# Top-k attention with a rational feed-forward: a cubic written as a line times a shifted square, weight bits on ScalarE, reciprocals on VectorE

## The chip, the core and the metric

The kernel runs on one core of a Trainium2 chip. The metric is device time in microseconds (us) of one launch. The core has five engines that each work through a fixed list of instructions in order: TensorE (PE in the profile, its weight loads PEld), VectorE (DVE), ScalarE (ACT), GpSimd (POOL) and SyncE (SP), which issues the transfers (DMA).

## What is computed

For 8 batches of 8 heads with 576 rows of 64, the attention keeps the 32 largest scores of each row; its output feeds a layer with a rational activation. The two weights arrive as float64.

```python
scores = scale * np.matmul(q, k.transpose(0, 1, 3, 2))
kth = np.partition(scores, -top_k, axis=-1)[..., -top_k:-top_k + 1]
scores = np.where(scores >= kth, scores, -1000000000.0)
scores = scores - np.max(scores, axis=-1, keepdims=True)
attn = np.exp(scores)
attn = attn / (np.sum(attn, axis=-1, keepdims=True) + 1e-09)
x = np.matmul(attn, v)                      # then laid out as 4608 x 512
h = x @ w_in                                # w_in 512 x 2048
h2 = h * h
h3 = h2 * h
P = a[0] + a[1] * h + a[2] * h2 + a[3] * h3
Q = 1.0 + np.abs(b[0]) * np.abs(h) + np.abs(b[1]) * h2
g = P / (Q + 1e-6)
out = g @ w_out                             # w_out 2048 x 512
```

## The kernel before

**Tiles.** The attention is cut into 288 tiles of 128 rows by 576 scores (32 of them hold the last 64 rows of two heads). A unit is two tiles, one for each head of a pair, or one such mixed tile; there are 160 units. For a tile TensorE computes the scores (L616), ScalarE copies them out of PSUM (`sb`, L623), VectorE folds the two halves into their maxima and minima (`hi`, L634, `lo`, L627) and takes the top 32 by repeated MAX and MATCH_REPLACE (L645, L653), ScalarE takes the exponentials (`e`, L684), and VectorE keeps those above the 32nd and sums them (`pr` and `ss`, L687). For a unit the sum then gets 1e-9 added (`guard`, L277 or L275 by engine), is inverted (`inverse`, L746, on GpSimd as a power of -1), is spread over 128 columns (`widen`, `rw`, L283 or L281), and is transposed with the probabilities on TensorE (L768, L770); the products with v (`av`, L794) are multiplied by it (L813).

**Feed-forward.** 256 rows make a chunk (18 of them), and a chunk takes 8 groups of 256 hidden columns. Each operand of a product is split in a high and a low part, and three products are added: `ph` (L943) for a group's hidden values, `po` (L1109) for the output. Between the two, a group's 128 x 512 values pass through ScalarE and GpSimd. There are two forms. The 15 first chunks (120 groups) use four evictions from PSUM by ScalarE (`square`, `p1`, `size`, `p3`), two GpSimd operations for the cubic (`p2`, L969, and `p4`, L975), and three ScalarE passes for 1/Q: the square of a shifted |h| (`rise`), Ln, and Exp of its negative. The 3 last chunks (24 groups, `y.late`) use three evictions and a Horner scheme, with `slope`, `curve`, `horner2`, `horner1` and `horner0` (L277, L1023, L1026, L1030 on VectorE; L1034, L1035 on GpSimd). Then both split the result into `g` (L277 or L275) and `gl` (L1007, GpSimd).

**Weights.** 32 blocks of 128 x 512 float64 are loaded as pairs of 32-bit words (`w_w`) while the attention is already running. For each half of a block ScalarE takes the sign of the high word (L422), VectorE shifts the high word into a PSUM tile (`high`, L427) and joins the top bits of the low word (`low`, L434), ScalarE takes the size (L440), GpSimd multiplies by the sign (L444), and the block is split in two (L460).

**Order.** A planner in the kernel (`Plan`) places every step: it holds lengths for each engine, keys for urgency (table `KEY`), and rings of buffers, and it writes the instructions down in the order in which its own clock starts them. Each engine then runs its list in order and waits where an input is not there. A second program for all data (`full`) follows behind a test of flags; it runs when `unfit` or one of the flags is above zero.

## Time and profile before

| | |
|---|---|
| median of 3 runs | 1566.55 us (1564.59 to 1568.24) |
| the profiled execution | 1566.08 us, of which the trace's span is 1564.3 us |
| busy: TensorE, its weight loads | 1416.2 us (91%), 1183.0 us (76%) |
| busy: VectorE | 1446.5 us (92%) |
| busy: ScalarE | 1306.3 us (84%) |
| busy: GpSimd | 1325.1 us (85%) |

Busy time is a union over an engine's instructions. Instructions of one engine overlap a little (the end of one is written back while the next runs), so a group's mean length is some hundredths of a microsecond above what it keeps the engine for.

### The profile page before, as it was taken

What the parts mean: (1) busy time and instruction counts of PE and PEld (TensorE: products, weight loads), DVE (VectorE), ACT (ScalarE), POOL (GpSimd) and SP (SyncE); (2) the same over time, 40 slices, a digit from 0 to 9 for tenths busy, and PEclk for the clock granted to TensorE, in tenths of its full rate; (3) what the DMA queues carried; (4) which work ended last, traced back from release to release, by engine and by line L of the source; (5) the groups of instructions that cost most, each with busy time, mean ns of one, the idle gap of its engine ahead of it and who ended that gap; (6) DMA issues with size and microseconds to landing.
All of it is one profiled execution on the core that took longest, in us unless ns stands there. A gap on an engine that the chain in (4) does not pass through costs nothing.

```text
span 1564.3 us, 32666 instructions
## 1 busy us (share of the span) xinstructions
PE 1416.2 (91%) x9729; PEld 1183.0 (76%) x9729; DVE 1446.5 (92%) x4548; ACT 1306.3 (84%) x2587; POOL 1325.1 (85%) x1893
## 2 busy tenths in 40 slices
PE   2547876998999999899999999999999999999998
PEld 1335655787788788788788888888888888887796
DVE  6998989999999999899999999999999999999773
...
GB/s 211 233 185 206 189 169 232 210 133 204 222 190 172 177 227 210 175 179 227 227 191 173 200 208 247 171 188 214 230 171 170 224 209 192 178 177 131 166 206 129
DMA packets 175004, 303.23 MB, mean 194 GB/s; under 512 B 26080, under 2 KB 80352, under 8 KB 174816
## 3 DMA queue, kind: packets, MB, share of 16 engines
...
q14 instruction: 108, 0.88, 0.2%
q0 software_dynamic: 64, 0.00, 0.0%
...
## 4 chain that ended last, share of the span: by engine, by line
PE 45%; DVE 16%; POOL 15%; ACT 9%; DMA 6%; issue 5%; SPq 3%; POOLq 0%; ACTq 0%; DVEq 0%
PE ph_m L943 13%; PE po_m L1109 12%; PE av L794 8%; PE s L616 5%; DVE m L645 5%; PE trp L768 4%; DVE hi L653 4%; DVE pr L687 2%; DMA wi_m<-win_l 2%; POOL ss L746 2%; DVE hi L634 2%; ACT sb L623 2%; DVE lo L627 1%; POOL gl_m L1007 1%; ACT p L780 1%
## 5 line engine op out<-in xcount | busy, mean ns | idle before, releaser
L645 DVE MAX8 m<-hi 128x8 f32<-128x288 f32 (+1 forms) x1152 | 500.6, 454 | 0.8
L653 DVE MATCH_REPLACE8 hi<-m,hi 128x288 f32<-128x288 f32 x864 | 380.2, 445 | 0.0
L943 PE MATMUL ph_m<-xh_m,win_h 128*128 128x256 f32 x1024 | 305.5, 298 | 4.3 <-ACT p L780 4.2
L943 PE MATMUL ph_m<-xh_m,wi_m 128*128 128x256 f32 x1024 | 292.1, 285 | 3.8 <-DMA wi_m<-win_l 3.8
L943 PE MATMUL ph_m<-xl_m,win_h 128*128 128x256 f32 x1024 | 290.5, 284 | 0.0
L768 PE MATMUL trp<-ident,pr 128*128 128x128 f32 x1312 | 227.6, 285 | 67.8 <-DVE pr L687 26.5
L780 ACT COPY p<-trp 128x512 f32<-128x512 f32 (+1 forms) x448 | 230.1, 519 | 39.9 <-PE trp L768 24.5
L768 PEld LDWEIGHTS trp<-ident,pr 128*128 128x128 f32 x1312 | 164.7, 145 | 108.7 <-ACT w_w L440 29.3
L687 DVE SCALAR_TENSOR_TENSOR pr<-sb,m,e 128x576 f32<-128x576 f32 x288 | 230.5, 800 | 2.6 <-ACT e L684 1.6
L684 ACT ACTIVATE e<-sb,st 128x576 f32<-128x576 f32 x288 | 219.1, 761 | 11.4 <-DVE pr L687 7.8
L623 ACT COPY sb<-s 128x576 f32<-128x576 f32 x288 | 186.6, 648 | 41.8 <-PE s L616 32.4
L1109 PE MATMUL po_m<-wout,g_m 128*128 128x512 f32 x512 | 217.9, 426 | 1.0 <-ACT ob_t L1127 1.0
L943 PEld LDWEIGHTS ph_m<-xh_m,win_h 128*128 128x128 f32 x1024 | 197.4, 193 | 14.6 <-ACT p L780 7.9
L1109 PE MATMUL po_m<-wout,gl_m 128*128 128x512 f32 x512 | 204.0, 399 | 3.7 <-POOL gl_m L1007 3.7
L1109 PE MATMUL po_m<-wl_m,g_m 128*128 128x512 f32 x512 | 203.7, 398 | 0.0
L943 PEld LDWEIGHTS ph_m<-xh_m,wi_m 128*128 128x128 f32 x1024 | 193.6, 189 | 4.4 <-DMA wi_m<-win_l 4.4
L943 PEld LDWEIGHTS ph_m<-xl_m,win_h 128*128 128x128 f32 x1024 | 194.8, 190 | 2.3
L794 PE MATMUL av<-p,vm 128*64 128x256 f32 (+1 forms) x1920 | 193.4, 351 | 3.4 <-ACT p L780 2.1
L1007 POOL TENSOR_TENSOR gl_m<-pa_m,g_m 128x512 fp32r<-128x512 f32 x128 | 168.2, 1314 | 4.5
L794 PEld LDWEIGHTS av<-p,vm 128*64 128x64 f32 x1920 | 114.3, 145 | 75.0 <-issue 17.1
L634 DVE TENSOR_TENSOR hi<-s,sb 128x288 f32<-128x288 f32 x288 | 128.6, 447 | 38.9 <-ACT sb L623 26.8
L969 POOL TENSOR_TENSOR pa_m<-pa_m,hh_m 128x512 f32<-128x512 f32 x112 | 144.9, 1294 | 21.2 <-ACT pa_m L966 20.8
(144 smaller groups left out, 3539.8 us busy)
## 6 DMA issues: line engine op xcount, KB each, us to landing
wl_m<-wout_l SPq DMA_DIRECT2D x256, 256.0 KB, 3.4
wi_m<-win_l SPq DMA_DIRECT2D x128, 512.0 KB, 4.2
...
q<-qx SPq DMA_DIRECT2D x128, 128.0 KB, 2.6
q<-qx SPq DMA_DIRECT2D x256, 64.0 KB, 2.1
...
```

Of the source, the lines that this page charges most:

```text
L623: nc.scalar.copy(t.sb, t.s[:, :, 0:HF])
L634: nc.vector.tensor_tensor(t.hi, t.s[:, 0, 0:HF], t.sb[:, 1], ALU.max)
L645: nc.vector.max(to, t.both if not full and o == 24 else getattr(t, src))
L653: nc.vector.match_replace(x, t.m[:, o : o + 8], x, NEG)
L684: nc.scalar.activation(t.e, t.sb, AF.Exp, scale=SCALE, bias=t.st)
L687: nc.vector.scalar_tensor_tensor(out=t.pr, in0=t.sb, scalar=t.kth, in1=t.e, op0=ALU.is_ge, op1=ALU.mult, accum_out=u.ss[:, t.h : t.h + 1],)
L768: nc.tensor.transpose(u.ps[i][:, c * P : (c + 1) * P], u.pr[:, x], ident)
L780: nc.scalar.copy(pair.pT[i][:, at].rearrange("p c n -> p (c n)"), u.ps[i][:, 0 : n * P])
L794: nc.tensor.matmul(pair.av[d, 0 : u.nq * len(pair.units)], lhs, x[:, 0, d] if u.mixed else x[:, 0] if lone else x, start=(c == 0), stop=(c ...
L943: nc.tensor.matmul(y.ph[:, f * NT : (f + 1) * NT], w, z[:, c, :], start=(c == 0 and i == 0), stop=(c == HP - 1 and i == 2),)
L1007: engine().tensor_tensor(out=tile_("gl", F32R), in0=y.pa, in1=y.g.bitcast(F32), op=ALU.subtract)
L1109: nc.tensor.matmul(o.po[i], z, w, start=(ff == 0 and n == 0), stop=(ff == NF - 1 and n == 2),)
```

## The change

1. **The cubic.** With a root r of the cubic found on the chip, P(h) = (a3 h - a3 r) ((h + t)^2 + f). A group has one eviction as a Square with a bias (`curve`), one as a line (`line`), one as |h| (`size`), and one step `cubic` = (curve + f) * line, which GpSimd does in two instructions (L1084, L1085) and VectorE could do in one. All 144 groups take this form; the late form is gone, and `slope`, `horner2`, `horner1`, `horner0` with it.
2. **Coefficients.** `add_coefficients` puts the root's Newton steps and a test of how well the form fits into the plan: 68 GpSimd instructions of one column, 11 on VectorE, 8 on ScalarE. The 11 one-column instructions that VectorE had for this at the start are gone.
3. **Weight bits.** `ends3` on ScalarE reads the low word as an unsigned number, scales it and adds 2, which leaves its top bits in place; VectorE's `merge` joins the shifted high word. The step `high` on VectorE is gone (64 instructions); ScalarE has 64 more of 128 x 256. The PSUM tile of the first eight blocks comes from another ring (`o` for `mm`), and a block takes three buffers for four.
4. **Reciprocals.** `inverse` is a RECIPROCAL on VectorE (160 instructions) for the power on GpSimd.
5. **Planner.** New lengths and keys, and small delays (`later`) that it assumes behind the guard, the reciprocal and loads. The products on TensorE and the transfers are the same in number.

```diff
@@ the weights
-                def high(i=i, place_bits=place_bits):
+                def ends3(i=i, place_bits=place_bits):
                     es, low, high, size_ = o.raw[i]
-                    nc.vector.tensor_scalar(
-                        place_bits(), high, 3, 0x40000000,
-                        op0=ALU.logical_shift_left, op1=ALU.bitwise_xor,
+                    nc.scalar.activation(
+                        place_bits().bitcast(F32), low.bitcast(U32), AF.Identity, scale=THREE, bias=toggle
                     )
-                def low(i=i):
+                def merge(i=i):
                     es, low, high, size_ = o.raw[i]
                     nc.vector.scalar_tensor_tensor(
-                        o.bits[i], low, 29, o.bits[i], op0=ALU.logical_shift_right, op1=ALU.bitwise_or
+                        o.bits[i], high, 3, o.bits[i], op0=ALU.logical_shift_left, op1=ALU.bitwise_xor
                     )
...
-                s2 = add("DVE", 0.33, high, [s1], key + 1, take=[bits_hold])
-                s3 = add("DVE", 0.36, low, [s2], key + 1)
+                s2 = add("ACT", act(256, 1), ends3, [ld], key + 1, take=[bits_hold])
+                s3 = add("DVE", 0.36, merge, [s1, s2], key + 1)
@@ the coefficients
+    def add_coefficients(key):
...
+        def over(o, x):
+            to("DVE", 0.16, lambda: nc.vector.reciprocal(o, x))
...
+        over(over_tilt, slope0)
+        ts((zero, a0, over_tilt, None, m, None))
+        for i in range(5):
+            value = (
+                (value0, zero, a3, a2, m, p), (value0, value0, zero, a1, m, p), (value0, value0, zero, a0, m, p),
+            )
+            ts(*value, (tilt, zero, slope2, slope1, m, p), (tilt, tilt, zero, slope0, m, p))
+            over(over_tilt, tilt)
+            ts((zero, value0, over_tilt, zero, m, p))
...
+        to("DVE", 0.16, lambda: nc.vector.tensor_tensor(unfit, unfit, outer, ALU.max))
+        return last[0]
@@ a unit's reciprocal
         def inverse():
-            x = u.ss[:, 0:nr]
-            if plan.at == "DVE":
-                nc.vector.reciprocal(x, x)
-            else:
-                nc.gpsimd.tensor_tensor(out=x, in0=x, in1=minus[:, 0:nr], op=ALU.pow)
+            nc.vector.reciprocal(u.ss[:, 0:nr], u.ss[:, 0:nr])
...
-        inv = add({**small(KEY["NM"]), "POOL": 0.27}, None, guard, [t1], key + KEY['URG'])
-        inv = add("DVE", 0.085, inverse, [inv], key + KEY['URG']) if full else add(
-            "POOL", KEY['PW'], inverse, [inv], key + KEY['URG'])
+        inv = add({**small(KEY["NM"]), "POOL": 0.27}, None, guard, [t1], key + KEY['URG'], later=0.12)
+        inv = add("DVE", 0.085, inverse, [inv], key + KEY['URG'], later=KEY['IL'])
@@ a group
+        def curve():
+            nc.scalar.activation(tile_("pa"), y.ph, AF.Square, bias=turn)
+        def line():
+            nc.scalar.activation(tile_("hh"), y.ph, AF.Identity, scale=a3, bias=near)
+        def cubic():
+            add_mult(y.pa, flat, y.hh)
...
+            e1 = add("ACT", act(512, 1), curve, [last, prev.e], ku, give=[mm], take=took)
+            s1 = add("ACT", act(512, 2), line, [e1], ku + 0.1, give=[mm])
+            e2 = add("ACT", act(512), size, [e1], ku + 0.2, give=[mm])
+            s3 = add(fused(512, *KEY['p2']), None, cubic, [s1, e1], k2 + 0.3, give=[th["hh"]])
+            s4 = add("ACT", act_sb(512, 2), rise, [e2], k2 + KEY['RI'])
```

Where instructions stand now, at three places. In the rows a line is that of its own kernel, and a name ends in batch, row block, pair and a buffer number.

**GpSimd, start of the program.** Behind the constants GpSimd had the first query block (`qx`), the first keys (`kh`, `kl`), and the first weights (`w_w0`, on lines L444 and L460):

```order
L277 TENSOR_SCALAR qx_0_0_0_145<-qx_0_0_0_145 128x256
L558 TENSOR_TENSOR qx_0_0_0_145<-qx_0_0_0_145 128x256
L277 TENSOR_SCALAR kh_0_0_166<-kl_0_0_149 128x576
L515 TENSOR_TENSOR kl_0_0_149<-kl_0_0_149,kh_0_0_166 128x576
L444 TENSOR_TENSOR w_w0_2_155<-w_w0_0_151,w_w0_2_155 128x256
L444 TENSOR_TENSOR w_w0_2_155<-w_w0_1_153,w_w0_2_155 128x256
L460 TENSOR_TENSOR w_w0_3_156<-w_w0_2_155,win_h_95 128x512
```

Now coefficients (`cf`, from the loaded `co`) stand ahead of the first keys and between all that follows:

```order
L485 TENSOR_SCALAR cf_73<-cf_73 128x1
L483 TENSOR_SCALAR cf_73<-co_70 128x1 x3
L281 TENSOR_SCALAR kh_0_0_162<-kl_0_0_131 128x576
L483 TENSOR_SCALAR cf_73<-co_70,cf_73 128x1
L588 TENSOR_TENSOR kl_0_0_131<-kl_0_0_131,kh_0_0_162 128x576
L485 TENSOR_SCALAR cf_73<-cf_73,co_70 128x1 x3
L485 TENSOR_SCALAR cf_73<-cf_73 128x1 x2
L281 TENSOR_SCALAR qx_0_0_0_154<-qx_0_0_0_154 128x256
L485 TENSOR_SCALAR cf_73<-cf_73 128x1
L631 TENSOR_TENSOR qx_0_0_0_154<-qx_0_0_0_154 128x256
L485 TENSOR_SCALAR cf_73<-cf_73,co_70 128x1 x3
L485 TENSOR_SCALAR cf_73<-cf_73 128x1 x2
```

Twelve coefficient instructions stand ahead of `kh` (the last four of them open this piece), and the query block has moved behind the keys.

**VectorE, start.** Before, the order was four weight instructions, the eleven for the coefficients, and then the first tile's `hi`. Now it is this, with `cf` the reciprocals of the root search:

```order
L489 RECIPROCAL cf_73<-cf_73 128x1 x5
L429 SCALAR_TENSOR_TENSOR w_w0_b0_184<-w_w0_0_156,w_w0_b0_184 128x256
L429 SCALAR_TENSOR_TENSOR w_w0_b1_193<-w_w0_1_158,w_w0_b1_193 128x256
L489 RECIPROCAL cf_73<-cf_73 128x1 x3
L707 TENSOR_TENSOR hi_0_0_0_246<-s_0_0_0_0_230,sb_0_0_0_0_239 128x288
L700 TENSOR_TENSOR lo_0_0_0_0_250<-s_0_0_0_0_230,sb_0_0_0_0_239 128x288
L718 MAX m_0_0_0_252<-hi_0_0_0_246 128x8
L489 RECIPROCAL cf_73<-cf_73 128x1
L726 MATCH_REPLACE hi_0_0_0_246<-m_0_0_0_252,hi_0_0_0_246 128x288
```

Eight reciprocals stand ahead of the first `hi`, each with its input from GpSimd, and a ninth two rows behind it.

**VectorE and GpSimd around one unit (batch 4, row block 1, pair 2).** Before, VectorE went from the last tile of the unit (`pr_4_1_2`) straight through the next tile:

```order
L687 SCALAR_TENSOR_TENSOR pr_4_1_2_12155,ss_4_1_2_12156<-sb_4_1_2_1_12145,m_4_1_2_12111,e_4_1_2_1_12231 128x576
L645 MAX m_4_0_3_12264<-hi_4_0_3_12236 128x8
L634 TENSOR_TENSOR hi_4_0_3_12236<-s_4_0_3_1_12259,sb_4_0_3_1_12277 128x288
L653 MATCH_REPLACE hi_4_0_3_12236<-m_4_0_3_12264,hi_4_0_3_12236 128x288
L627 TENSOR_TENSOR lo_4_0_3_1_12333<-s_4_0_3_1_12259,sb_4_0_3_1_12277 128x288
L645 MAX m_4_0_3_12264<-hi_4_0_3_12236 128x8 x2
L653 MATCH_REPLACE hi_4_0_3_12236<-m_4_0_3_12264,hi_4_0_3_12236 128x288 x2
```

Now the unit's reciprocal stands between the next tile's operations:

```order
L760 SCALAR_TENSOR_TENSOR pr_4_1_2_12048,ss_4_1_2_12049<-sb_4_1_2_1_12006,m_4_1_2_11994,e_4_1_2_1_12125 128x576
L718 MAX m_4_0_3_12150<-hi_4_0_3_12123 128x8
L707 TENSOR_TENSOR hi_4_0_3_12123<-s_4_0_3_1_12144,sb_4_0_3_1_12161 128x288
L726 MATCH_REPLACE hi_4_0_3_12123<-m_4_0_3_12150,hi_4_0_3_12123 128x288
L700 TENSOR_TENSOR lo_4_0_3_1_12203<-s_4_0_3_1_12144,sb_4_0_3_1_12161 128x288
L718 MAX m_4_0_3_12150<-hi_4_0_3_12123 128x8 x2
L815 RECIPROCAL ss_4_1_2_12049<-ss_4_1_2_12049 128x2
L726 MATCH_REPLACE hi_4_0_3_12123<-m_4_0_3_12150,hi_4_0_3_12123 128x288 x2
```

On GpSimd the unit's guard and power (both `ss_4_1_2`) and its factor `rw` stood so:

```order
L670 TENSOR_TENSOR fl_4_11123<-hi_4_1_2_12088,m_4_1_2_12111 128x2
L277 TENSOR_SCALAR g_m3_0_7_12302<-pa_m3_0_7_12125 128x512
L277 TENSOR_SCALAR ss_4_1_2_12156<-ss_4_1_2_12156 128x2
L277 TENSOR_SCALAR qx_4_1_2_12267<-qx_4_1_2_12267 128x256
L746 TENSOR_TENSOR ss_4_1_2_12156<-ss_4_1_2_12156,minus_91 128x2
L558 TENSOR_TENSOR qx_4_1_2_12267<-qx_4_1_2_12267 128x256
L283 TENSOR_SCALAR rw_4_1_2_12348<-ss_4_1_2_12156 128x128
```

and now the guard stands behind a 128 x 512 split (`xl_m3_2`), and the power is gone:

```order
L743 TENSOR_TENSOR fl_4_10994<-hi_4_1_2_11968,m_4_1_2_11994 128x2
L281 TENSOR_SCALAR qx_4_1_2_12106<-qx_4_1_2_12106 128x256
L971 TENSOR_TENSOR xl_m3_2_12113<-x_m3_2_10166,xh_m3_2_12112 128x512
L281 TENSOR_SCALAR ss_4_1_2_12049<-ss_4_1_2_12049 128x2
L631 TENSOR_TENSOR qx_4_1_2_12106<-qx_4_1_2_12106 128x256
L287 TENSOR_SCALAR st_4_0_3_12151<-m_4_0_3_12150 128x1
L287 TENSOR_SCALAR rw_4_1_2_12225<-ss_4_1_2_12049 128x128
```

VectorE's reciprocal has six instructions between it and the unit's last `pr`, and all of VectorE's list stands behind its wait.

On TensorE, behind the last `av`, there were 360 instructions of `ph` and 213 of `po`; there are now 384 and 216. In the three last chunks GpSimd does L1084, L1085, the product with 1/Q (L1066) and `gl` for every group, and VectorE nothing.

## Rows read from the trace of the kernel before

**Rows 1.** Three stretches: busy PE, PEld, DVE, ACT, POOL; PEclk, DMA, GB/s.
```profile
0.00:300.00 300.00, 191.07 (x1082) 140.96 (x1083) 261.36 (x836) 198.55 (x434) 225.47 (x360) 0.81 0.68 204
300.00:1450.00 1150.00, 1122.39 (x8011) 951.86 (x8010) 1114.65 (x3630) 1049.29 (x2051) 1035.71 (x1477) 0.99 0.65 194
1450.00:1564.00 114.00, 102.77 (x638) 90.15 (x638) 70.51 (x84) 58.49 (x105) 63.91 (x57) 0.98 0.52 167
```

**Rows 2.** The same view of the steady stretch.
```profile
400.00:1400.00 1000.00, 980.04 (x7042) 831.81 (x7042) 969.38 (x3162) 917.27 (x1790) 905.33 (x1307) 1.00 0.66 199
```

**Rows 3.** The same stretch, VectorE's L687 alone (two records to a tile).
```profile
400.00:1400.00 1000.00, 169.56 (x420) 1.00 0.66 199
```

**Rows 4.** Who waited for whom: VectorE (total us, times, longest).
```profile
DVE hi L634 <- ACT sb L623: 26.8, 44, 1.9
...
DVE hi L634 <- POOL fl L670: 6.3, 11, 1.4
```

**Rows 5.** The chain that ended last, its end (start us, length).
```profile
1460.29 2.31 PE av L794 x20
...
1539.63 2.88 PE ph_m L943 x24
1542.50 13.25 PE po_m L1109 x57
```

**Rows 6.** GpSimd in order of time, start (start us, length, what).
```profile
2.39 0.58 POOL L297 DMA_DIRECT2D co<-in_moe_b_dram  x1
...
9.83 0.67 POOL L277 TENSOR_SCALAR kh<-kl 128x576 fp32r<-128x576 f32 x1 [4.25 <-DMA kl<-in_qk_dram]
10.58 1.40 POOL L515 TENSOR_TENSOR kl<-kl,kh 128x576 fp32r<-128x576 f32 x1
```

**Rows 7.** DMA issues of the first 30 us (KB each, us to landing).
```profile
co<-in_moe_b_dram POOLq DMA_DIRECT2D x1, 1.0 KB, 5.8
```

**Rows 8.** VectorE in order of time, start.
```profile
15.67 0.16 DVE L307 RECIPROCAL sq<-sq 128x1 f32<-128x1 f32 x1 [1.90 <-ACT sq L305]
...
18.37 0.15 DVE L316 TENSOR_SCALAR sq<-sq 128x1 f32<-128x1 f32 x1
18.44 0.45 DVE L634 TENSOR_TENSOR hi<-s,sb 128x288 f32<-128x288 f32 x1
```

**Rows 9.** Groups by line and shape (busy us, mean ns, idle before): weights.
```profile
L427 DVE TENSOR_SCALAR w_w_b<-w_w 128x256 int32<-128x256 int32 x64 | 26.5, 419 | 26.1 <-DMA w_w<-in_moe_w_in_dram 11.5 <-ACT x_m L811 7.9 <-ACT p L780 4.1
...
L422 ACT ACTIVATE w_w<-w_w 128x256 f32<-128x256 f32 x64 | 25.6, 435 | 13.3 <-DMA w_w<-in_moe_w_in_dram 11.8 <-DMA w_w<-in_moe_w_out_dram 1.5
```

**Rows 10.** The same view: the reciprocal and the row factor.
```profile
L746 POOL TENSOR_TENSOR ss<-ss,minus 128x2 f32<-128x2 f32 x128 | 90.2, 704 | 5.1 <-ACT ss L275 2.7 <-PE trp L768 0.3
...
L281 ACT ACTIVATE rw<-ss 128x128 f32<-128x128 f32 x69 | 21.9, 318 | 17.8 <-POOL ss L746 17.6
...
L746 POOL TENSOR_TENSOR ss<-ss,minus 128x1 f32<-128x1 f32 x32 | 17.7, 553 | 0.6 <-ACT st L281 0.2
```

**Rows 11.** The same view: GpSimd's operations, and its smallest.
```profile
L969 POOL TENSOR_TENSOR pa_m<-pa_m,hh_m 128x512 f32<-128x512 f32 x112 | 144.9, 1294 | 21.2 <-ACT pa_m L966 20.8
...
L283 POOL TENSOR_SCALAR st<-m 128x1 f32<-128x1 f32 x198 | 38.2, 193 | 15.1 <-DVE m L645 14.2
...
L1034 POOL TENSOR_SCALAR pa_t<-pa_t,co 128x512 f32<-128x512 f32 x13 | 9.1, 698 | 0.2
```

**Rows 12.** The same view: ScalarE's operations of a group.
```profile
L966 ACT ACTIVATE pa_m<-ph_m,co 128x512 f32<-128x512 f32 x128 | 101.6, 794 | 0.0
...
L972 ACT ACTIVATE h_m<-ph_m,co 128x512 f32<-128x512 f32 x112 | 89.7, 801 | 0.0
...
L959 ACT ACTIVATE hh_m<-ph_m 128x512 f32<-128x512 f32 x112 | 67.9, 606 | 5.9 <-PE ph_m L943 5.4
```

**Rows 13.** VectorE by line and shape, from 1445 us on.
```profile
L1023 DVE TENSOR_TENSOR va_m<-hh_m,va_m 128x512 f32<-128x512 f32 x16 | 20.9, 1303 | 1.0
...
L1030 DVE SCALAR_TENSOR_TENSOR pa_m<-pa_m,co,va_m 128x512 f32<-128x512 f32 x16 | 12.1, 755 | 3.2 <-ACT va_m L998 1.7
```

More of the change, by code (lines that the diff above doesn't have):

```diff
@@ L13 @@
 I32 = mybir.dt.int32
+U32 = mybir.dt.uint32
 BF16 = mybir.dt.bfloat16
@@ L64, in fits @@
             need[h.tag] = need.get(h.tag, 0) + 1
-        return all(self.left[t] >= n + (self.SPARE if n > 3 else 0) for t, n in need.items())
+        return all(self.left[t] >= n + (self.SPARE if n > 2 else 0) for t, n in need.items())
     def grab(self, h):
@@ L72, in grab, with add @@
         self.left[h.tag] -= 1
-    def add(self, eng, length, emit, after=(), key=0.0, take=(), give=(), crit=False, alt=1.0, kind="f"):
+    def add(self, eng, length, emit, after=(), key=0.0, take=(), give=(), crit=False, alt=1.0, kind="f", later=0.0):
         s = Obj()
-        s.alt, s.kind = alt, kind
+        s.alt, s.kind, s.later = alt, kind, later
         s.alts = {eng: length} if length is not None else dict(eng)
@@ L129, in run @@
                     if e == "PE":
+                        s.length *= next((x for t, x in self.CLOCK if now < t), 1.0)
                         if s.kind == "r" != self.kind:
@@ L143, in run @@
                     for d in s.next:
-                        lag = max(self.LAG[e][a] for a in d.alts)
-                        d.ready = max(d.ready, s.end + lag)
+                        lag = max(self.LAG[e][a] + (a != e) * KEY['SLACK'].get(a, 0.0) for a in d.alts)
+                        d.ready = max(d.ready, s.end + lag + d.later)
                         d.wait -= 1
@@ L533, in add_kv @@
         ld = add("SP", dma(1, P * S), load, key=k2, take=[rhold])
-        s = add(one(S, 0, KEY['XH']), None, high_part, [ld], k2 + 1)
+        s = add(one(S, 0, KEY['XH']), None, high_part, [ld], k2 + 1, later=KEY['LD'])
         s = add(two(S, *KEY['LP']), None, low_part, [s], k2 + 1)
@@ L1053, in add_group @@
                            (split + wdep + [wi] if first else []) + [last], key,
-                           take=[mm] + ([th[n] for n in ("hh", "va", "pa", "h")] if KEY['TH'] else []) if first else [], give=[wih] + ([xs] if f == FG - 1 and c == HP - 1 else []), kind="r")
+                           take=[mm] + (held if early else []) if first else [], give=[wih] + ([xs] if f == FG - 1 and c == HP - 1 else []), kind="r")
         k2 = key + KEY['EW']
         ku = key + KEY['EU']
-        fours = [th[n] for n in ("hh", "va", "pa", "h")]
@@ new lines, in add_group @@
+        took = [] if early else held
+        if full:
+            mm.users = 4
+            e1 = add("ACT", act(512), square, [last, prev.e], ku, give=[mm], take=took)
+            s1 = add("ACT", act(512, 2), p1, [e1], ku + 0.1, give=[mm])
+            e2 = add("ACT", act(512, 1), size, [e1], ku + 0.2, give=[mm])
+            s3 = add("ACT", act(512, 2), p3, [e1], ku + 0.3, give=[mm])
+            s2 = add(two(512, *KEY['p2']), None, p2, [s1, e1], k2 + 0.3)
+            s4 = add(one(512, 1, KEY['Q0']), None, q0, [s2], k2 + 0.35)
+            s4 = add(two(512, *KEY['Q1']), None, q1, [e2, s4], k2 + 0.4, give=[th["hh"]])
+            s3 = add(two(512, *KEY['p4']), None, p4, [s3, s2], k2 + 0.6, give=[th["h"]])
+        else:
+            mm.users = 3
+            e1 = add("ACT", act(512, 1), curve, [last, prev.e], ku, give=[mm], take=took)
[3 more added lines that the diff above has]
+            s4 = add("ACT", act_sb(512, 2), rise, [e2], k2 + KEY['RI'])
@@ L1080, in add_group @@
         prev.e = e1
-        l1 = add("ACT", act_sb(512, 0 if full and not y.late else 1), log, [s4], k2 + 0.6)
+        l1 = add("ACT", act_sb(512, 0 if full else 1), log, [s4], k2 + 0.6)
         l2 = add("ACT", act_sb(512), inverse, [l1], k2 + 0.7)
-        if y.late:
-            gg = add(fused(512, *KEY['B3']), None, horner0, [l2, s3], k2 + 0.8, alt=0, give=[th["va"]])
-        else:
-            gg = add(two(512, *KEY['ratio']), None, ratio, [l2, s3], k2 + 0.8, give=[th["va"]])
+        gg = add(two(512, *KEY['ratio']), None, ratio, [l2, s3], k2 + 0.8, give=[th["va"]])
```

152 lines of the change are left out of this document (83 added, 69 removed).

## The prediction

> **What bounds the kernel now.** I read the stretches first, then the steady one closely, then who waits for whom, then the end of the chain. Three stretches differ [rows 1]. In the first 300 us weights are prepared beside the attention: TensorE is busy for 191 us at a mean granted clock of 0.81, VectorE for 261. From 300 to 1450 us TensorE (1122 of 1150) and VectorE (1115) are both nearly full, ScalarE (1049) and GpSimd (1036) nine tenths. In the last 114 us the attention is over, TensorE works off products (103 us) and VectorE is busy for 70.5 with the late form of the groups.
>
> In the steady 1000 us [rows 2] VectorE is busy for 969. Line L687 leaves two records for each tile and has 420 there [rows 3]: 210 tiles, one each 4.76 us, of which VectorE works 4.62. So VectorE sets the pace of the attention, and all that it is given or relieved of before 1450 us counts. What it waits for is mostly ScalarE's copy of the scores, 26.8 us, and GpSimd's release of `hi`, 6.3 us [rows 4]. After the last `av` (1460.3 us) the chain is TensorE's: 24 `ph` in 2.88 us, and 57 `po` in 13.25 us at the end, so 2.79 us for the 12 of a group [rows 5]. The end therefore comes when VectorE has finished the attention, plus the products left then.
>
> TensorE is a second candidate: 980 us busy of those 1000 [rows 2], against 832 of its weight loads. The Trainium skill (Perfetto Trace Analysis, Identifying the Most-Contended Engine) holds matmul busy time to be no measure of how full TensorE is, because pipelined matmuls overlap in a trace, and would have weight loads judged instead. By that rule there is a sixth to spare, VectorE paces, and the sum below stands; by the busy row there is nothing to spare, and only the start and the end of that sum are left. I follow the pace in rows 3 and keep the other case as a rival.
>
> **The change part by part**, summed along VectorE's list and then TensorE's end.
>
> *Start, +6 us.* The coefficient `b` is issued at 2.4 us [rows 6] and lands 5.8 us later [rows 7], at 8.2. Twelve one-column GpSimd instructions now stand ahead of `kh`, at 0.19 each [rows 11], with three reciprocals (0.16 [rows 8]) and four small ScalarE steps, for which I take 0.19 too, between them: 2.3 + 0.5 + 0.8 = 3.6, so `kh` starts at 11.8 at the earliest, where it started at 9.83 [rows 6]. Then come 0.67 and 1.40 for the keys [rows 6], seven small ones (1.3), and the query block, half the size of the operations of rows 11 (0.35 + 0.65): its transfers can start at 16.2, where the keys' could at 11.98. By that the scores are 4.2 us late. VectorE's eighth reciprocal stands ahead of the first `hi`: 17 more small instructions (3.2), two joins of half the size (1.3) and one whole (1.3) bring it to 22.0, again 3.6 behind the 18.44 of [rows 8]; hand-overs between engines come on top. Bounds 4 and 9, as the dozen hand-overs are free or take as long as a small instruction; 6 taken. The eleven old small instructions end within these 18.4.
>
> *Weights, -29 us.* L427 goes: 64 of 419 ns [rows 9]. A record overlaps the next by 0.08 (the 0.15 of L316 keeps VectorE for 0.07 [rows 8]), so 64 x 0.34 = 21.8. In front of L427 VectorE stood for 26.1 us; 11.5 are the first load, 14.6 waits in which mostly ScalarE held the PSUM tile [rows 9]. The tile is now taken by ScalarE itself, but `merge` waits for `ends3`; I give back half, 7.3. Bounds: all 14.6 gained (-36), or as much waited in the new place (-8). `ends3` costs ScalarE 64 times 0.43 to 0.53: L422's 435 ns [rows 9], with half of what two per-partition operands add to a 128 x 512 eviction (606 to 794 ns [rows 12]). These 31 us lie in a stretch where ScalarE idles for 101 [rows 1]; without that cover, the copies behind them would hold VectorE.
>
> *Reciprocals, +13 and +10 us.* 160 on VectorE. A column takes 0.16 [rows 8], less the overlap 0.08: 13 us (bounds 0.07, 11 us, and the whole 0.16, 26). Before, the power kept GpSimd for 90.2 + 17.7 = 108 us [rows 10]. The new wait is for the guard on GpSimd or ScalarE, and VectorE's whole list stands behind it. Six instructions stand between a unit's last `pr` and its reciprocal, at 4.62 us for the dozen of a tile [rows 2, 3] some 2.2 us; the guard has one 1.29 us operation ahead of it at worst, and 0.19 of its own [rows 11], so it comes too late only where GpSimd runs 0.7 us behind the planner's clock. The nearest row for such a hand-over is the old one: ScalarE's 69 `rw` waited 17.6 us for GpSimd's power [rows 10], 0.255 us each. At that price it is 41 us; at none, 0. I take a quarter, 0.06 each, 10 us, since the planner now leaves a gap there.
>
> *Relief of GpSimd and ScalarE, -14 us.* In 120 groups two operations of 1.294 become one of 0.698 and one of 1.294 [rows 11]: 72 us less; the power 108 less. In the last 24 groups GpSimd gets 24 x (0.698 + 2 x 1.294) = 79 us where it had some 59 (37 of 1.29, 16 of 0.70); the coefficients cost 68 x 0.19 = 13. Together -147. ScalarE loses the 801 ns eviction, and its 606 ns square gets an operand, some 0.70 [rows 12]: 120 x 0.71 = 85 us less; the late groups get about 1.0 us each more (24), `ends3` 31: -30. These engines set no pace, so this counts only as VectorE's waits for them: it idles 35 us between 300 and 1450 [rows 1]. Bounds 0 and -35; two fifths taken, because many copies are late through TensorE, whose work is unchanged.
>
> *End, +4 us.* Behind the last `av` there are 24 `ph` and 3 `po` more: 2.88 + 3 x 0.23 = 3.6 [rows 5]. VectorE's 70.5 us there [rows 1] move to engines that must keep up with TensorE's 2.88 + 2.79 = 5.67 us a group. GpSimd needs 0.70 + 3 x 1.294, and 0.63 where it also makes `g`: 4.6 to 5.2.
>
> Sum: 6 - 29 + 13 + 10 - 14 + 4 = -10, from the profiled 1566 us, which is also the median of the runs: **1556 us**.
>
> **The rivals.** *The waits dissolve.* With GpSimd at four fifths nearly all of the 35 us goes (31), and no reciprocal waits: 17 + 10 us below the forecast, and 2 for 0.07: 1527. For it: VectorE's waits are short ones for engines that are relieved [rows 4]. Against it: a full TensorE delays the scores, whoever copies them.
>
> *The reciprocals stall VectorE.* If each waits as ScalarE's `rw` did, 41 us instead of 10: 1587. It decides between faster and slower from an average wait of (10 + 10)/160 = 0.13 us on. For it: GpSimd's operations of 1.3 us cannot be broken off, and its list is 0.9 full. Against it: the six instructions between.
>
> *TensorE paces.* Then the VectorE terms vanish in the middle, and the early lead is lost while TensorE works off the same products: start and end alone are left, in part absorbed: 1566 to 1573.
>
> *GpSimd bounds the end.* The Trainium skill (GPSIMD Engine Reference, Engine selection) advises VectorE over GpSimd for elementwise work, GpSimd being about twice as slow with two inputs. Rows here show 1.29 us on GpSimd [rows 11], and on VectorE, beside GpSimd, 0.755 for L1030 but 1.303 for L1023, both with two inputs [rows 13]; so the trace bears the rule out for one line of the two. As a mechanism it needs GpSimd to enter the end with a backlog: 16 groups x 5.2 and 4 for a split make 87 us against TensorE's 95 behind the last `av`, so it decides from 8 us on and would cost about that: 1564.
>
> *The test refuses the form*, and the second program runs too: over 3000 us. With the coefficients that the reference's setup draws, five Newton steps from -a0/a1 settle after two, and each bound holds with a factor above 7.
>
> **How the numbers follow.** Forecast 0.42 (own range 1546 to 1565), waits dissolve 0.20, stalls 0.20, TensorE paces 0.12, GpSimd's end 0.05, refused 0.01. The likeliest gives 1556. With half of the second and half of the third case left out, and the last, the range is 1529 to 1588, 0.21 outside. A change of 0.2% (3 us) is about what can be told from none. Faster: 0.38 + 0.20 + 0.02 + 0.02 = 0.62; slower: 0.19 + 0.05 + 0.01 = 0.25; same 0.13.
>
> **What the profile of after would show.** Start: the first `hi` at about 24 us and GpSimd's `kh` at 12. Weights: VectorE's idle time in front of `merge` at 7 us beyond the first load, and by 300 us three or four more tiles than before. Reciprocals: a line of 160 at 0.16 us with 10 us of idle time in front. Relief: GpSimd's busy time near 1180, ScalarE's near 1275, VectorE's idle time for L634's successor below 20 us, a steady pace of 4.7 us. End: TensorE without gaps behind the last `av`. The prediction is wrong if idle time in front of the reciprocal exceeds 20 us, if the pace falls to 4.65, or if tiles come no earlier at 400 us.

## The result and the profile after

The changed kernel takes **1525.24 us** (median of 4 runs, 1521.02 to 1526.23) where the kernel before takes 1567.39 on the same chip (1564.59 to 1568.98): ratio 0.9728, 95% interval 0.9704 to 0.9752. Forecast were 1556 us in a range of 1529 to 1588. The sign was right, the gain is four times the one forecast, and the time lies below the range; the rival in which the waits dissolve (1527) comes nearest. The profiled execution took 1526.23 us, with a span of 1524.4.

Its three stretches, in the columns of [rows 1] and cut where its attention ends:

```profile
0.00:300.00 300.00, 197.99 (x1201) 149.06 (x1202) 257.54 (x864) 231.14 (x525) 236.09 (x420) 0.86 0.70 213
300.00:1411.00 1111.00, 1096.59 (x7885) 940.82 (x7884) 1095.12 (x3697) 984.29 (x1898) 867.35 (x1321) 0.99 0.65 198
1411.00:1524.00 113.00, 103.81 (x646) 91.05 (x644) 2.08 (x8) 75.63 (x125) 92.51 (x91) 0.98 0.54 174
...
400.00:1400.00 1000.00, 986.87 (x7130) 846.93 (x7130) 985.38 (x3328) 883.64 (x1707) 778.83 (x1194) 0.99 0.65 199
```

The last `pr` starts at 1410.6 us instead of 1452.5, and the last stretch is as long as it was, with as many TensorE instructions (646; 638 in [rows 1]). In the middle VectorE idles for 16 us (35 before) and TensorE for 14 (28 before). In the steady 1000 us (last line; [rows 2]) there are 428 records of `pr`, two to a tile: 4.67 us a tile where [rows 3] gave 4.76.

For whom VectorE waited, whole span (total us, times, longest), as in [rows 4], without the 100.7 us that it stands at the end of the program:

```profile
...
DVE cf L489 <- POOL cf L485: 15.3, 5, 4.3
DVE ss L815 <- POOL ss L281: 10.4, 20, 3.3
DVE cf L489 <- ACT cf L499: 9.6, 1, 9.6
DVE hi L707 <- ACT sb L696: 7.2, 7, 2.3
DVE w_w_b L429 <- ACT w_w_b L423: 5.0, 8, 1.3
DVE ss L815 <- ACT ss L279: 3.5, 5, 1.5
...
DVE hi L707 <- POOL fl L743: 1.2, 3, 0.5
```

The 26.8 us for `sb` and 6.3 for `fl` have shrunk to 7.2 and 1.2; new are 13.9 in front of the reciprocals (`ss`) and the coefficients (`cf`). The start, VectorE in order of time, to be held against [rows 8]:

```profile
24.73 0.16 DVE L489 RECIPROCAL cf<-cf 128x1 f32<-128x1 f32 x1 [3.60 <-POOL cf L485]
28.35 0.17 DVE L489 RECIPROCAL cf<-cf 128x1 f32<-128x1 f32 x1 [3.46 <-POOL cf L485]
28.43 0.44 DVE L707 TENSOR_TENSOR hi<-s,sb 128x288 f32<-128x288 f32 x1
```

The first `hi` comes at 28.43 us, 10 later than before, and it stands behind reciprocals whose inputs GpSimd delivers late. The end is TensorE's as in [rows 5], now without a gap of note.

### The profile page after: what moved, and what is told of

It reads as the page before. It is cut to its first block, busy times and chain, and to the rows that moved or that the text cites. A ratio compares the mean times of both kernels' runs of the same rounds, so it can differ in the third digit from the quotient of the medians.

```text
span 1524.4 us, 32556 instructions
## 1 busy us (share of the span) xinstructions
PE 1398.4 (92%) x9729; PEld 1180.9 (77%) x9729; DVE 1354.7 (89%) x4567; ACT 1291.1 (85%) x2546; POOL 1196.0 (78%) x1830
## 3 DMA queue, kind: packets, MB, share of 16 engines
q8 instruction: 80, 1.31, 0.4%
## 4 chain that ended last, share of the span: by engine, by line
PE 68%; DVE 9%; POOL 7%; ACT 7%; DMA 5%; issue 3%; SPq 1%; POOLq 0%; ACTq 0%; DVEq 0%
PE ph_m L1010 19%; PE po_m L1156 17%; PE av L863 10%; PE s L689 7%; PE trp L837 7%; PE ph_t L1010 3%; DVE m L718 2%; PE po_t L1156 2%; DMA wi_m<-win_l 2%; DVE hi L726 2%; DVE pr L760 2%; PE s L686 1%; ACT p L849 1%; POOL cf L485 1%; PE trp L839 1%
## 5 line engine op out<-in xcount | busy, mean ns | idle before, releaser
L757 ACT ACTIVATE e<-sb,st 128x576 f32<-128x576 f32 x288 | 215.9, 750 | 22.8 <-DVE pr L760 17.4
L1066 POOL TENSOR_TENSOR pa_m<-pa_m,va_m 128x512 f32<-128x512 f32 x128 | 165.2, 1291 | 75.9 <-ACT va_m L1063 73.7
L863 PE MATMUL av<-p,vm 128*64 128x256 f32 (+1 forms) x1920 | 188.4, 345 | 8.2 <-ACT w_w L435 5.1
L1085 POOL TENSOR_TENSOR pa_m<-pa_m,hh_m 128x512 f32<-128x512 f32 x128 | 165.3, 1291 | 18.6 <-ACT hh_m L1091 7.8
```

What stands on the lines that cost most here:

```text
L757: nc.scalar.activation(t.e, t.sb, AF.Exp, scale=SCALE, bias=t.st)
L863: nc.tensor.matmul(pair.av[d, 0 : u.nq * len(pair.units)], lhs, x[:, 0, d] if u.mixed else x[:, 0] if lone else x, start=(c == 0), stop=(c ...
L1085: nc.gpsimd.tensor_tensor(out=x, in0=x, in1=z, op=ALU.mult)
```

## The experiments

All are compared with the kernel before by the ratio that was timed beside it. The changed kernel itself was timed twice: 0.9728 (above) and 0.9713 (e17_after_again). Differences in us are between the medians of the table. The kernels were timed in several groups, each with the kernel before beside it (its medians are 1566.1 to 1569.6), so by the ratios a difference comes out up to some 3 us otherwise; where it matters both are given. Whenever arithmetic or a number changes, the planner writes the whole order anew; differences of some 3 us are therefore not interpreted. A tile "comes" when its `pr` starts. In the table "attention" is the start of the last `pr`; "left" are TensorE's instructions from there to the end; "idle" is VectorE's idle time from 300 us to that `pr`; the last three columns are waits between 300 and 1400 us: VectorE's for `sb` and `fl`, VectorE's in front of the reciprocals, and GpSimd's for transfers in front of its first instruction on a query or key block (`qx`, `kh`).

| kernel | us | ratio (95%) | attention | left | idle | sb, fl | guard | GpSimd, transfers |
|---|---|---|---|---|---|---|---|---|
| before | 1567.4 | 1 | 1452.5 | 634 | 35.4 | 26.7 | - | 16.9 |
| changed | 1525.2 | 0.9728 (0.9704-0.9752) | 1410.6 | 646 | 15.9 | 5.1 | 8.7 | 10.0 |
| e1_old_plan | 1558.5 | 0.9925 (0.9903-0.9948) | 1445.7 | 641 | 36.2 | 4.7 | 28.0 | 54.5 |
| e7_new_plan | 1563.8 | 0.9968 (0.9941-0.9994) | 1421.6 | 794 | 15.1 | 10.6 | - | 5.0 |
| e2_power | 1520.8 | 0.9690 (0.9663-0.9716) | 1399.0 | 698 | 14.9 | 12.9 | - | 8.2 |
| e3_bits | 1549.5 | 0.9871 (0.9850-0.9892) | 1435.9 | 646 | 19.2 | 8.5 | 8.4 | 7.9 |
| e4_cubic | 1535.0 | 0.9775 (0.9751-0.9799) | 1411.6 | 723 | 15.4 | 7.8 | 5.9 | 2.5 |
| e5_no_gap | 1536.9 | 0.9799 (0.9747-0.9851) | 1422.2 | 651 | 22.3 | 4.8 | 15.8 | 4.4 |
| e6_old_plan_gap | 1551.5 | 0.9885 (0.9833-0.9938) | 1442.0 | 644 | 41.6 | 8.5 | 29.9 | 68.3 |
| e8_late_coef | 1528.6 | 0.9747 (0.9696-0.9799) | 1410.9 | 647 | 15.8 | 7.7 | 6.9 | 11.7 |
| e9_old_loads | 1549.6 | 0.9896 (0.9848-0.9944) | 1433.4 | 647 | 36.4 | 13.4 | 19.7 | 41.4 |
| e10_old_pace | 1531.4 | 0.9777 (0.9743-0.9812) | 1418.1 | 646 | 20.2 | 5.1 | 11.1 | 11.1 |
| e11_old_ranks | 1535.2 | 0.9809 (0.9775-0.9844) | 1413.9 | 646 | 18.0 | 10.8 | 5.5 | 9.4 |
| e12_spread_coef | 1529.9 | 0.9771 (0.9733-0.9808) | 1407.4 | 694 | 17.9 | 8.2 | 7.3 | 10.5 |
| e13_no_lead | 1544.0 | 0.9856 (0.9812-0.9900) | 1422.1 | 669 | 27.0 | 7.3 | 18.2 | 47.1 |
| e14_old_loads_lead | 1531.0 | 0.9760 (0.9722-0.9798) | 1415.0 | 646 | 15.7 | 6.5 | 7.3 | 6.6 |
| e15_old_plan_lead | 1546.4 | 0.9869 (0.9829-0.9908) | 1434.3 | 636 | 25.9 | 10.0 | 13.2 | 10.5 |
| e16_long_gap | 1529.8 | 0.9774 (0.9730-0.9819) | 1414.9 | 649 | 17.9 | 13.4 | 2.5 | 7.5 |
| e17_after_again | 1523.1 | 0.9713 (0.9696-0.9729) | 1412.1 | 646 | 17.7 | 7.1 | 8.7 | 11.2 |
| e18_power_again | 1522.3 | 0.9702 (0.9686-0.9718) | 1400.6 | 698 | 15.8 | 13.1 | - | 6.9 |

**Arithmetic or order?** e1_old_plan gives the new arithmetic the old numbers of the order (gathered here from the lines of its edit; `-` is the changed kernel, `+` this one):

```diff
-'KL': -16.348, 'VL': -15.549, 'LD': 1.5, 'ROOM': {'v': 2, 'wl': 4}
+'KL': -3.492, 'VL': -7.485, 'LD': 0.0, 'ROOM': {'v': 1, 'wl': 5}
-'T': 5.448, 'MOE': 132.644, 'PACE': 15.382, 'MS': 0.313, 'AV': 4.855, 'PT': -11.194, 'WG': 5.575
+'T': 5.009, 'MOE': 108.806, 'PACE': 10.749, 'MS': 1.337, 'AV': 5.345, 'PT': -12.13, 'WG': 4.406
-'EX': 7.004, 'EW': 1.494, 'RI': 11.198, 'ALT': {'ACT': 0.388, 'POOL': 0}, 'LOOK': 0.27
+'EX': -19.047, 'EW': 16.974, 'RI': 7.015, 'ALT': {'ACT': 0.389, 'POOL': 0.024}, 'LOOK': 0.3
-'IL': 0.3, 'TN': 2, 'p2': ('POOL', 'DVE')   later=0.12   CLOCK = ((150.0, 1.2), (300.0, 1.05))
+'IL': 0.0, 'TN': 0, 'p2': ('POOL',)   later=0.0   CLOCK = ()
-"DVE": 0.069 + n / 480 (two), 0.069 + n / 650 (fused)
+"DVE": dve(n) (two), 0.069 + n / 870 (fused)
```

> The changed kernel with all its new arithmetic, but ordered by the numbers of the kernel before: the keys PT, AV, MOE, LOOK, T, KL, EX, EW, ALT, WG, PACE, MS, VL, RI, the room of v and wl and the planner's lengths are the old ones, and the new delays (LD, IL, 0.12), TN and CLOCK are nought. Theory A (relief: the cheaper form and the power taken off GpSimd dissolved VectorE's waits, whatever the order): at most 1535 us, with VectorE's idle time between 300 us and the last pr below 25 us. Theory B (order: the new numbers dissolved them): 1548 us or more, with idle time there near the 35 us of the kernel before. Between the two, both have a share.

1558.46 us. Of the 42 us only 9 remain (12 by the ratio), although each instruction that the change saves is still saved. Theory A has fallen, but not because relief does nothing: VectorE's waits for `sb` and `fl` are as small (4.7 us) as in the changed kernel. Their place is taken by the reciprocals, and GpSimd stands in front of transfers (VectorE's waits, then GpSimd's instruction by line and shape with its idle time, 300 to 1400 us):

```profile
DVE ss L815 <- POOL ss L281: 25.6, 37, 1.9
DVE hi L707 <- ACT sb L696: 4.1, 7, 1.3
DVE ss L815 <- ACT ss L279: 2.4, 3, 1.3
...
L281 POOL TENSOR_SCALAR qx<-qx 128x256 fp32r<-128x256 f32 x47 | 19.1, 407 | 56.3 <-DMA qx<-in_qk_dram 32.5 <-DMA out_dram<-ob_m 11.9 <-DMA wl_m<-wout_l 6.9
```

How the one leads to the other is seen at 742 us of the same kernel, GpSimd and then VectorE in order of time:

```profile
741.17 1.31 POOL L1085 TENSOR_TENSOR pa_t<-pa_t,hh_t 128x512 f32<-128x512 f32 x1
745.66 0.41 POOL L281 TENSOR_SCALAR qx<-qx 128x256 fp32r<-128x256 f32 x1 [3.19 <-DMA qx<-in_qk_dram]
...
746.88 1.30 POOL L1066 TENSOR_TENSOR pa_t<-pa_t,va_t 128x512 f32<-128x512 f32 x1
...
748.29 0.63 POOL L281 TENSOR_SCALAR g_t<-pa_t 128x512 fp32r<-128x512 f32 x1
748.99 0.19 POOL L281 TENSOR_SCALAR ss<-ss 128x2 f32<-128x2 f32 x1
```

```profile
745.95 0.79 DVE L760 SCALAR_TENSOR_TENSOR pr<-sb,m,e 128x576 f32<-128x576 f32 x1
...
747.47 0.44 DVE L726 MATCH_REPLACE8 hi<-m,hi 128x288 f32<-128x288 f32 x1
749.22 0.17 DVE L815 RECIPROCAL ss<-ss 128x2 f32<-128x2 f32 x1 [1.31 <-POOL ss L281]
```

GpSimd stands 3.19 us until the query block has landed. Then it works off what has gathered, and the guard comes last, at 748.99; its input, the last `pr`, had been complete since 746.7. VectorE, which has run out of instructions ahead of the reciprocal, stands for 1.31 us.

e7_new_plan is the other half: the old arithmetic, with the new numbers (KL to LOOK above without p2, the lengths, CLOCK and LD).

> The kernel before, with all its old arithmetic, ordered by the new numbers (all keys that both kernels have save p2, the room of v and wl, the planner's lengths, CLOCK, LD; the gaps have no place in it, as the reciprocal is GpSimd's power). If the new order is of use whatever the arithmetic (theory O): 1535 to 1545 us, with VectorE's waits for sb below 12 us. If it is of use only to the new arithmetic, as theory G has it: 1558 to 1575 us.

1563.84 us: the time is theory G's, but the attention is theory O's. It does end 31 us earlier, with `sb` and `fl` at 10.6 us, but with 794 TensorE instructions left instead of 634, so the last stretch takes 141 us instead of 112. The middle and the end in the columns of [rows 1], and the same for e4_cubic (below):

```profile
300.00:1422.00 1122.00, 1099.55 (x7902) 933.01 (x7902) 1106.85 (x3624) 1056.03 (x2079) 998.27 (x1418) 1.00 0.66 198
1422.00:1563.00 141.00, 129.28 (x793) 112.69 (x791) 81.55 (x88) 72.87 (x129) 92.47 (x76) 0.97 0.52 166
```

```profile
300.00:1412.00 1112.00, 1099.22 (x7928) 942.15 (x7927) 1096.58 (x3702) 1037.28 (x2001) 933.03 (x1342) 1.00 0.65 200
1412.00:1536.00 124.00, 115.86 (x722) 102.16 (x721) 1.35 (x8) 84.53 (x139) 102.89 (x100) 0.98 0.54 171
```

The last stretch is TensorE's: 129.28 of 141 us. Arithmetic alone is worth 9 us (12 by the ratio), order alone 4 (5), both 42 (43).

**Which arithmetic?** Three kernels take one part out of the changed kernel. e2_power:

```diff
-            nc.vector.reciprocal(u.ss[:, 0:nr], u.ss[:, 0:nr])
...
+                nc.gpsimd.tensor_tensor(out=x, in0=x, in1=minus[:, 0:nr], op=ALU.pow)
```

> The changed kernel with the reciprocals back on GpSimd as powers of -1, all else as in it. VectorE loses 12 us of its own and the 13.9 us that it waited for the guards; GpSimd gets about 108 us, from 1196 to 1304. Theory A: the part of the relief that was the power (108 of 193 us of GpSimd time, so about 18 of 30 us of waits) comes back, and ScalarE's or GpSimd's rw waits for the power again: 1512 to 1525 us. Theory B: the waits stay away, and 1500 us is reached. If the reciprocals on VectorE were the better choice by themselves, over 1528.

1520.79 us, in the interval of theory A, but with a reason of neither: without the 160 reciprocals the attention ends 11.6 us earlier, and 52 more instructions are left. e18_power_again repeated it beside the changed kernel (e17_after_again, no edit).

> The changed kernel once more, unaltered, on the same chip and in the same rounds as e18_power_again: 1525 us, ratio to the kernel before 0.970 to 0.976. It sets the scale for differences of a few us between runs of other calls.

> Run e2_power once more, unaltered (the changed kernel with its reciprocals as powers on GpSimd), beside the changed kernel. If the reciprocals on VectorE cost more than they give (12 us of its time and 8.7 us of waits after 300 us, against 86 us of GpSimd time), it is faster by 3 to 7 us: ratio 0.966 to 0.970. If e2_power's 4.4 us were only the difference between two calls: within 2 us of the changed kernel.

1523.08 and 1522.31 us: no difference. Moving the reciprocal to VectorE neither cost nor gave time here. The Trainium skill (GPSIMD Engine Reference, Engine selection) advises VectorE rather than GpSimd for elementwise work; these runs show no gain from that for 160 instructions of one or two columns.

e3_bits puts the weight bits back (`high` and `low` on VectorE for `ends3` and `merge`):

```diff
-                s2 = add("ACT", act(256, 1), ends3, [ld], key + 1, take=[bits_hold])
-                s3 = add("DVE", 0.36, merge, [s1, s2], key + 1)
+                s2 = add("DVE", 0.33, high, [s1], key + 1, take=[bits_hold])
+                s3 = add("DVE", 0.36, low, [s2], key + 1)
```

> The changed kernel with the weight bits back as two VectorE instructions of each half block (high and low in place of ends3 on ScalarE and merge on VectorE). By the term of the prediction, VectorE paces while weights are prepared: 64 x 0.34 = 22 us and some 10 us of waits come back: 1550 to 1557 us, and tile 64 comes about 22 us later than in the changed kernel. Rival: TensorE, ScalarE or the transfers pace that stretch and VectorE has room: below 1538 us, tile 64 less than 10 us later.

1549.53 us, just below the interval and 24 more than the changed kernel (22 by the ratios); tile 64 comes at 384.7 us instead of 362.4. In the new order the term of the prediction (29) holds, 5 us smaller.

e4_cubic keeps the old form in the first 120 groups:

```diff
+        elif old:                                # x.n < 15
+            e1 = add("ACT", act(512), square, [last, prev.e], ku, give=[mm], take=took)
+            s1 = add("ACT", act(512, 2), p1, [e1], ku + 0.1, give=[mm])
...
+            s3 = add(two(512, *KEY['p4']), None, p4, [s3, s2], k2 + 0.6, give=[th["h"]])
```

> The changed kernel with the old form of the cubic (square, p1, p2, p3, p4) in the first 120 groups and the new form in the last 24, all else as in it. GpSimd gets 120 x 0.6 = 72 us (1268), ScalarE some 85 us (1376). Theory A: VectorE waits for ScalarE's sb and GpSimd's fl again, by 15 to 30 us: 1540 to 1555 us. Theory B: 1525 to 1532 us, VectorE's waits for sb stay below 12 us in sum.

1535.04 us, between the two intervals. Theory B is right on the waits (`sb` 5.9 us, idle time 15.4), and yet it costs 10 us (7 by the ratios): the attention ends as early as in the changed kernel, with 723 instructions left instead of 646 (rows above). ScalarE (1037 of 1112) and GpSimd (933) get fewer groups done beside the attention. So the cheaper form pays, but as groups finished earlier, not as VectorE's waits.

**Which numbers of the order?** e5_no_gap takes out IL (0.3 us that the planner leaves behind the reciprocal) and the 0.12 us behind the guard; e6_old_plan_gap puts both into e1_old_plan.

> The changed kernel with only the two gaps taken out that its planner leaves around the guard (0.12 us) and before what follows the reciprocal's issue (IL, 0.3 us); all other numbers stay new. Run e1_old_plan had neither gap, and there VectorE stood 32.6 us in front of the reciprocals (27.0 for GpSimd's guard, 5.6 for ScalarE's) where it stands 13.9 us in the changed kernel. Theory G (the gaps hide the guards; without them the rival of the prediction, reciprocals that stall VectorE, comes true): waits in front of the reciprocal of 25 us or more, 1536 to 1546 us. Theory O (the other numbers of the order do it): waits below 18 us, at most 1530 us.

> Run e1_old_plan (the new arithmetic under the old order) with those two gaps put back and nothing else. Theory G: the 19 us of waits go again, 1537 to 1543 us, and what is left to the 1525 us of the changed kernel is the first 64 tiles (13 us later in e1_old_plan). Theory O: 1550 to 1558 us.

1536.88 us, with 21.5 us in front of the reciprocals in the whole span (13.9 in the changed kernel): the gap is worth some 12 us here, by fewer waits than expected. In the old order it gives 7, all in the first 64 tiles, and the guard waits stay at 29.9: theory G doesn't explain e1_old_plan. The other numbers were then put back group by group, each group a pair of lines of the diff above (e9: the first pair, e10: the second, e11: the third).

> The changed kernel with the old numbers of the loads alone: KL and VL (keys and values loaded later), one buffer for v, five for wl, no LD; all other numbers new. The new order is worth 33 us to the new arithmetic (1558.5 us in e1_old_plan against 1525.2) of which the gaps at the guard hold some 12. Three groups of numbers are left. If the loads hold most of the other 20 us, because scores or av waited for transfers: 1540 us or more, with TensorE's idle time after 300 us near the 31 us of e1_old_plan. If they hold none: 1522 to 1530 us.

> The changed kernel with the old numbers of the pace alone: T, MOE, PACE, MS, AV, PT, WG (how closely tiles, groups, values, transposes and weight blocks follow each other in the order); all others new. If the pace holds most of the other 20 us: 1540 us or more, with TensorE's idle time after 300 us near 30 us; if it holds none: 1522 to 1530 us.

> The changed kernel with the old ranks alone: EX (the exponential, which the old order puts ahead of nearly all else on ScalarE), EW and RI (the later steps of a group), ALT and LOOK; all others new. If ScalarE's copies of the scores were late because exponentials stood ahead of them, VectorE's waits for sb rise from 7 us to over 20 and the time to 1535 to 1545 us; if not, 1522 to 1530 us.

1549.57, 1531.38 and 1535.17 us. The loads carry 24 us and bring the signature of e1_old_plan back, GpSimd's 41 us in front of transfers included; pace and ranks carry some 6 to 10 each (e10_old_pace lies between its two intervals), and `sb` rises only to 9.0 in e11_old_ranks, so its time is in the interval but not by the wait that was expected. What is left of the group is LD, 1.5 us that the planner adds to a load's length before it places the first reader, or the earlier loads:

```diff
-'LD': 1.5
+'LD': 0.0
```

> The changed kernel with LD alone at 0 instead of 1.5 us, the lead that the planner allows a transfer of keys or queries before it places the instruction that reads it. In e9_old_loads GpSimd stood 17.8 us between 300 and 1400 us in front of the first instruction on a query block (qx) until its transfer landed, in e1_old_plan 44.4 us, in the kernel before 12.0, in the changed one not once, and the guards and st behind it came late. Theory L (the lead is the cause): such waits of 12 us or more, VectorE's waits for guards above 18 us, 1540 to 1550 us. Theory K (loading keys and values earlier, with two buffers for v, is the cause): no such rise, 1522 to 1530 us.

> Run e9_old_loads (old KL and VL, one buffer for v, five for wl) with LD put back to 1.5 us. Theory L: 1522 to 1532 us, no waits of GpSimd for qx. Theory K: 1540 to 1552 us as in e9_old_loads.

> Run e1_old_plan (the new arithmetic in the old order, 1558.5 us) with LD at 1.5 us and nothing else of the new numbers. Theory L: GpSimd's 44 us of waits for qx go and with them most of VectorE's waits for guards (27 us): 1535 to 1542 us. Theory K: 1552 to 1560 us.

1544.02, 1530.95 and 1546.43 us. (The "not once" of these texts was read from the longest rows only; the full list gives the changed kernel 10.0 us for `qx` and `kh`, 5.2 of them for the block's own load.) The first two are in theory L's intervals. e15_old_plan_lead lies between those of L and K: GpSimd's time in front of transfers falls from 54.5 to 10.5 us, as L has it, but only half of the waits for guards go (28.0 to 13.2). LD is worth 19 us with the new loads, 19 with the old, 12 in the old order (20, 21 and 9 by the ratios); KL, VL and the buffers give 6, which the intervals of e14_old_loads_lead and the changed kernel do not tell from nothing. The same rows as for e1_old_plan, from e13_no_lead and then from e15_old_plan_lead (its second row is of the view of the waits):

```profile
DVE ss L815 <- POOL ss L281: 17.9, 31, 1.5
...
L281 POOL TENSOR_SCALAR qx<-qx 128x256 fp32r<-128x256 f32 x41 | 16.7, 407 | 44.7 <-DMA qx<-in_qk_dram 28.0 <-DMA wl_m<-wout_l 7.0 <-DMA out_dram<-ob_m 4.1
```

```profile
DVE ss L815 <- POOL ss L281: 11.7, 21, 1.6
...
POOL qx L281 <- DMA qx<-in_qk_dram: 2.8, 4, 1.5
```

**Attempts at a better version.** e8_late_coef starts the chain of coefficients later, e12_spread_coef spreads it, e16_long_gap sets IL to 0.8.

```diff
+            if emit is magnitudes:
+                last[0].ready = KEY['CA']        # e8: 50.0, e12: 8.5; CF 60 in both
...
-            to("POOL", 0.19 * len(ops), emit)
+            to("POOL", 0.35 * len(ops), emit)    # e12: one step of 0.32 for each op
```

> The changed kernel with the chain of coefficients put off: its first step may start at 50 us of the planner's time instead of 0, with a lower rank (60 for 15), and GpSimd's one-column instructions are counted as 0.35 us instead of 0.19. The chain is needed by the first curve at 158 us. If the 10 us that the first hi came late are on the path: first hi at 18 to 20 us, tile 64 at 352 to 356 us instead of 362, and 1515 to 1519 us. If they are absorbed while the weights are prepared (tile 16 came at 120.6 us in the kernel before and at 121.8 in the changed one, although it began 10 us later): 1522 to 1527 us.

> The changed kernel with the chain of coefficients as single steps of 0.32 us in the planner's eyes, of a lower rank (60), from 8.5 us of its time, so that keys, queries and scores go ahead of them and each fills a hole of GpSimd; nothing else differs. In e8_late_coef the chain lay on GpSimd in blocks between 81 and 122 us, and VectorE lost there what it had won at the start. If those blocks were to blame: first hi at 18 to 20 us, tile 64 at 350 to 356 us, 1513 to 1520 us. If the start is absorbed whatever the place of the chain: tile 64 at 360 to 365 us, 1522 to 1528 us.

> The changed kernel with a gap of 0.8 us instead of 0.3 between the reciprocal and what uses it in the planner's eyes (IL), as an attempt at a better version. With no gap at all (e5_no_gap) it took 11.7 us more. If a longer gap goes on hiding guards, waits in front of the reciprocal fall from 13.9 to below 9 us and the time to 1515 to 1521 us; if 0.3 us was already enough, 1522 to 1530 us.

1528.57, 1529.93 and 1529.77 us: none is better. In e8_late_coef the first `hi` starts at 17.92 us and tile 16 comes 15 us earlier (107.1), but by tile 48 nothing is left (290.4 against 289.0). In e12_spread_coef tile 64 is 5 us earlier (357.3), and 48 more instructions are left at the end. So neither turns an earlier start into time. In e16_long_gap the guard waits between 300 and 1400 us fall to 2.5 us, but in the whole span only from 13.9 to 10.2, where below 9 were expected, and `sb` and `fl` take 13.4 instead of 5.1.

## Why the prediction was wrong, step by step

**The step that failed** is the relief, -14 us, and with it the fifth point of the change: the planner's new numbers had no term in the sum. Where the time went is seen from the start of tile 64's `pr` and of the last `pr`, in the kernel before, in the changed one and in e1_old_plan:

```profile
384.63 0.79 DVE L687 SCALAR_TENSOR_TENSOR pr<-sb,m,e 128x576 f32<-128x576 f32 x1
1452.53 0.81 DVE L687 SCALAR_TENSOR_TENSOR pr<-sb,m,e 128x576 f32<-128x576 f32 x1
...
362.36 0.81 DVE L760 SCALAR_TENSOR_TENSOR pr<-sb,m,e 128x576 f32<-128x576 f32 x1
1410.64 0.81 DVE L760 SCALAR_TENSOR_TENSOR pr<-sb,m,e 128x576 f32<-128x576 f32 x1
...
375.69 0.80 DVE L760 SCALAR_TENSOR_TENSOR pr<-sb,m,e 128x576 f32<-128x576 f32 x1
1445.71 0.81 DVE L760 SCALAR_TENSOR_TENSOR pr<-sb,m,e 128x576 f32<-128x576 f32 x1
```

By tile 64 the changed kernel is 22 us ahead, where start and weights add up to -23. From there to the last `pr` it gains another 20, where reciprocals and relief add up to +9. So it is in the middle that the sum failed. I sized the relief by how much less ScalarE and GpSimd have to do, took two fifths of VectorE's 35 idle us, and let the reciprocals wait for 10. The busy times fell nearly as said (GpSimd's to 1196 us, ScalarE's to 1291; 1180 and 1275 forecast), but what that is worth hangs on the order. In the old order the same arithmetic gains 9 us by tile 64 and loses 2 in the middle: there the waits for `sb` and `fl` fall by more than I said (26.7 to 4.7 us), the reciprocals wait 28 us and not 10, and the two about cancel. That its gain of 9 is so near to the -10 of the sum is luck, since its parts are others. The 33 us between e1_old_plan and the changed kernel are the order's, 12 to 19 of them (9 to 21 by the ratios) the lead LD. I looked for engines that are too full; what made GpSimd late was that it stood in front of transfers, with the guards queued behind. [Rows 6] show such a wait (4.25 us in front of `kh`), and the kernel before has 16.9 us of them in the middle.

None of the three signs named at the end of the prediction came (13.9 us in front of the reciprocals, a pace of 4.67, tile 64 earlier): they tested the terms of the sum, not the one that was missing. The rival in which the waits dissolve came nearest partly by luck: it lets the reciprocals wait for nothing, and it has VectorE's idle time go by relief alone, where e1_old_plan still has 36.2 us of it.

**Start, +6:** it came 10 us later, above the bound of 9, since GpSimd's one-column instructions with operands from columns take some 0.40 us each in a chain and not 0.19. In e8_late_coef 15 us won at tile 16 are gone by tile 48; in e12_spread_coef 5 us are still there at tile 64 but not at the end. What the late start itself costs isn't separated from the place of the chain.

**Weights, -29:** right in kind; in the new order 5 us too large (e3_bits gives 24). In the old order it isn't seen whole, as tile 64 of e1_old_plan comes only 9 us earlier. Tile 48 of the changed kernel comes at 289.0 us instead of 308.8, four tiles earlier as said, and the waits in front of `merge` are 5.0 us where I left 7.3. (The bound of -8 should read -7: 21.8 less 14.6.)

**Reciprocals, +13 and +10:** right as sizes (160 records of 0.156 us, each 0.075 to the next instruction, 12.0; waits 13.9 in the whole span) and wrong as a cost of time: without them the attention ends 11.5 us earlier, half of the 23, but with 86 us more on GpSimd and 52 more products left the time is the same (e18_power_again beside e17_after_again). The rival that they stall VectorE is what happens without LD and the gap.

**End, +4:** +2 (113.8 us from the last `pr` to the end, before 111.8), TensorE without gaps as said. What I missed is that the end is a second account: what the attention gains can come back as products left over (e4_cubic, e7_new_plan, e18_power_again).

**TensorE paces** was given 0.12. In the changed kernel it is busy for 1096.6 of the middle 1111 us and 103.8 of the last 113: behind 300 us it idles 24 us, where it idled 39 before. By these busy rows little is left to win there. No run takes work off TensorE, so whether VectorE or TensorE sets the pace behind 300 us isn't told apart; that an earlier attention so often came back as products left fits TensorE too.

Which numbers of the order make up the rest of the 33 us was tried only by groups. Taken out one by one (19, 6, 12, 6 and 10 us) they come to 53, so they overlap; CLOCK, TN and the lengths weren't tried alone. How much of the earlier attention in e7_new_plan is work merely put off isn't separated from waits saved.
